# The second quarter of the first tokens: cast during the DMA on GpSimd's queue, or fetched in float32 by SyncE and cast by GpSimd

## The chip, the cores and the metric

The kernel runs on one core of a Trainium2 chip. The metric is the device time of one execution in microseconds; the median of 3 runs of the kernel before is 680.97 us (680.66 to 681.43). A core has a matrix engine (TensorE, PE in the profile; its weight loads are PEld), a vector engine (VectorE, DVE), a scalar engine (ScalarE, ACT), GpSimd (POOL) and SyncE (SP), which only issues DMAs here. All run beside each other, each in its own program order, and wait for each other by semaphores. On chip there are SBUF, 128 partitions of working memory, and PSUM, into which TensorE writes.

## What is computed

A softmax over seven taps for each of eight heads weighs a causal convolution along the sequence; its result goes through a two-layer network with a leaky ReLU.

```python
w = exp(weight - max(weight)); w = w / (sum(w) + 1e-9)          # [8 heads, 7 taps]
x_pad = concat(zeros(B, 6, D), x)                               # x: [8, 4096, 192] float32
out[b, s, h, :] = sum_k w[h, k] * x_pad[b, s + k, h, :]         # a head has 24 of 192 channels
h = out.reshape(32768, 192) @ w_in                              # w_in [192, 2048]
y = maximum(0.01 * h, h) @ w_out                                # w_out [2048, 192], y float32
```

## The kernel before

The tokens are taken in blocks of 512 positions of two batch rows at once (NBLK = 32 blocks). The convolution wants channels on the partitions, so x is brought into a transposed layout, `xt`: 64 channels of one batch row on the lower 64 partitions, the same channels of the other row on the upper 64, for each of three groups of channels (NCH = 3, CH = 64). For each group of tokens there follow the convolution into `yt` (VectorE, L222 and L228; for the first tokens partly TensorE with diagonal matrices, L259), mm1 (`w_in` against `yt`, L507) into PSUM, the leaky ReLU by ScalarE into `g` (L515), and mm2 (`g` with `w_out`; L525 for the first two blocks, L588 after) with its evacuation and output DMA. The program order is written out by hand: mm2 of earlier tokens stands between the mm1 steps of later ones, and VectorE makes the next group's `yt` in the meantime.

The first block's tokens go in halves, so that TensorE can begin early: `groups` has four parts of 256 positions (the parts q = 0 to 3 of the helpers; parts 0 and 1 are block 0), then whole blocks. How a part comes into `xt` differs:

- Part 0: SyncE fetches it in float32 into `x_nat` (L142, two DMAs, one for each `s`, 128 positions). ScalarE and VectorE cast it into `x_half[0]` (`cast_first`, L155), in which the 64 channels of both batch rows lie side by side, and six matmuls against the identity transpose it (L181).
- Parts 1 and 2: two DMAs each on GpSimd's queue, which cast to bfloat16 on the way, into `x_rows[q]` (L145). The two batch rows lie apart there, so `transpose_first` takes 64 columns at a time: twelve transposes (L167). VectorE copies the result from PSUM into `xt` (`evac_first`, L195).
- Part 3: six DMAs on GpSimd's queue (L149), then DMA transposes on SyncE's queue (L199).

Later blocks: six casting DMAs each on GpSimd's queue (L96), then DMA transposes on SyncE's (L114).

GpSimd's program order at the start: the selection matrix; `w_in` rows 0 to 127 of the first half of the columns (L316, `load_w_in(0, 0)`); the identity; `load_w_in(0, 128, near)`; part 1 of x; `load_w_in(0, 128, far)`; the two loads of the second half of `w_in`; part 2 of x; the two halves of `w_out` (L350); the taps for VectorE, `wk` (L445, L446); part 3; block 2. SyncE's: part 0; then, at 18.12 us, the DMA transposes of part 3; then outputs and further transposes.

VectorE's order around the change: evacuation of part 1's transposes (L195), a spreading copy of `w_in` (L326), the first three jobs of part 1's convolution of channel group 1 (L222, L228, which read `wk`), then the spreading of the second half of `w_in` (`spread_down(1)`, L322; `spread_up`, L326), then the further jobs. The spreading copies put rows of `w_in` on the partitions where mm1 wants them. In mm1 of the very first step (`wide`), `transpose_first(1)` stands between the channel groups 1 and 2 (L501, L502): TensorE goes on to group 2 only behind part 1's transposes.

`sync(ins, after, why)` (L78) makes one instruction wait for another.

Of the kernel before, what the change touches and what calls it, by code (L numbers as in the profile page):

```python
# [10 lines left out]
FP32 = mybir.dt.float32  # L11
BF16 = mybir.dt.bfloat16
# [3 lines left out]
def kernel(  # L16
# [8 lines left out]
    nc = tc.nc  # L25

    B, S, D = x.shape
# [8 lines left out]
    CH = 64  # L36
    NCH = D // CH
# [3 lines left out]
    HS = SUB // 2  # L41
    NFC = F // 128
# [3 lines left out]
    RUN = 4  # L46
# [10 lines left out]
    const_pool = ctx.enter_context(tc.tile_pool(name="const", bufs=1))  # L57
    stage_pool = ctx.enter_context(tc.tile_pool(name="stage", bufs=2))
# [17 lines left out]
    x_nat, x_bf, xt = {}, {}, {}  # L76

    def sync(after, first, why):  # L78
        tc.add_manual_dep(
            after.ins, first.ins.name,  # L80
            mybir.DependencyInfo(
                mybir.DependencyClass.Sync, mybir.DependencyReason.DATA
            ),
            reason=why,
        )
# [36 lines left out]
    def new_xt(rp):  # L122
        xt[rp] = xt_pool.tile([128, NCH, HALO + S], BF16, name="xt")
        nc.vector.memset(xt[rp][:, :, 0:HALO], 0.0)
# [3 lines left out]


    x_half = {  # L130
        q: const_pool.tile([128, NCH, HS, 2, CH], BF16, name=f"x_half{q}") for q in (0, 3)
    }
    x_rows = {
        q: const_pool.tile([128, 2, HS, D], BF16, name=f"x_rows{q}") for q in (1, 2)
    }

    def load_first(q):
        rows = x[0:2, q * HT : (q + 1) * HT, :].rearrange("e (s p) d -> p e s d", s=HS)
        if q == 0:
            x_nat[q] = stage_pool.tile([128, 2, HS, D], FP32, name="x_nat")  # L140
            for s in range(HS):
                nc.sync.dma_start(out=x_nat[q][:, :, s], in_=rows[:, :, s])  # L142
        elif q in x_rows:
            for e in range(2):
                nc.gpsimd.dma_start(out=x_rows[q][:, e], in_=rows[:, e])  # L145
        else:
            for c in range(NCH):
                for e in range(2):
                    nc.gpsimd.dma_start(  # L149
                        out=x_half[q][:, c, :, e, :],  # L150
                        in_=rows[:, e, :, c * CH : (c + 1) * CH],
                    )

    def cast_first(q, s, copy, e=slice(0, 2)):
        copy(  # L155
            out=x_half[q][:, :, s, e, :],
            in_=x_nat[q][:, e, s, :].rearrange("p e (c k) -> p c e k", c=NCH),
        )
# [3 lines left out]
    def transpose_first(q, mid=None):  # L162
        if q:
            t = psum_o.tile([128, HS, NCH, 128], BF16, name="ptr", tag="po")
            for s, c in product(range(HS), range(NCH)):
                for e in range(2):
                    nc.tensor.transpose(  # L167
                        out=t[e * CH : (e + 1) * CH, s, c, :],
                        in_=x_rows[q][:, e, s, c * CH : (c + 1) * CH],
                        identity=ident,  # L170
                    )
            ptr[q] = [t[:, s] for s in range(HS)]
            return
        ts = [
            psum_o.tile([128, NCH, 128], FP32, name=f"ptr{s}", tag="po") for s in range(HS)
        ]
        for s, t in enumerate(ts):
            if s and mid is not None:
                mid()
            for c in range(NCH):  # L180
                nc.tensor.matmul(  # L181
                    out=t[:, c, :],
                    lhsT=x_half[q][:, c, s, :, :].rearrange("p e k -> p (e k)"),
                    rhs=ident,
                    start=True,
                    stop=True,
                )
        ptr[q] = ts
# [46 lines left out]
    def y_of(grp, c):  # L235
        blk, t0, T = grp
        if blk not in yt:
            yt[blk] = yt_pool.tile([128, NCH, ST], BF16, name="yt")
        return yt[blk][:, c, t0 : t0 + T]
# [47 lines left out]
    w9 = const_pool.tile([H, K + 1], FP32, name="w9")  # L287
    nc.scalar.dma_start(out=w9[:, 0:K], in_=weight)  # L288
    load_first(0)

    ones = nc.const_aps.tensor(1.0, [128, ST], BF16)
# [7 lines left out]
    for sign, off in ((1, 0), (-1, GRP - 1)):  # L299
        nc.gpsimd.affine_select(  # L300
            out=sel[:, :, 0, :], in_=sel[:, :, 0, :], compare_op=mybir.AluOpType.is_ge,
# [12 lines left out]
    def load_w_in(n, rows, cols=slice(0, WF)):  # L314
        ps, slot = ((0, 128), 0) if rows == 0 else ((0, CH), 2)
        nc.gpsimd.dma_start(  # L316
            out=w_in[n][ps[0] : ps[1], slot, cols],
            in_=moe_w_in[rows : rows + ps[1], n * WF + cols.start : n * WF + cols.stop],
        )
# [17 lines left out]
    ident = const_pool.tile([128, 128], BF16)  # L337
    make_identity(nc, ident)
    load_w_in(0, 128, near)
    load_first(1)  # L340
    load_w_in(0, 128, far)
    for rows in (0, 128):
        load_w_in(1, rows)
    load_first(2)


    w_out = const_pool.tile([128, NFC, D], BF16)
    for h in range(2):
        cs = slice(h * NFC // (2 * RUN), (h + 1) * NFC // (2 * RUN))
        nc.gpsimd.dma_start(  # L350
            out=w_out.rearrange("p (c i) d -> p c i d", i=RUN)[:, cs],
            in_=moe_w_out.rearrange("(c p i) d -> p c i d", p=128, i=RUN)[:, cs],
        )


    wa = psum_h.tile([128, 2, ST], FP32, name="warm", tag="ph")
# [1 line left out]
    def warm(n, cols=HT, to=wa[:, 0]):  # L358
# [10 lines left out]
        out=nmax, in_=w9[:, 0:K], axis=mybir.AxisListType.X,  # L369
# [3 lines left out]
        out=w9[:, 0:K], in_=w9[:, 0:K], func=mybir.ActivationFunctionType.Exp,  # L373
# [18 lines left out]
    def select(out, parts):  # L392
# [9 lines left out]
    select(wps_hm, slice(0, 2))  # L402
    wps_hm = wps_hm[:, :, 0]
    new_xt(0)
    cast_first(0, 0, nc.scalar.copy)
    cast_first(0, 1, nc.scalar.copy, slice(0, 1))
    cast_first(0, 1, nc.vector.tensor_copy, slice(1, 2))
    taps = const_pool.tile([128, NCH, 2, K + 1, 2], BF16, name="taps")
    nc.vector.tensor_copy(
        out=taps, in_=wps_hm[..., None].to_broadcast([128, NCH, 2, K + 1, 2])  # L410
# [5 lines left out]
    def diag_wide(c, p):  # L416
# [8 lines left out]

    warm(1, 192)
    transpose_first(0, lambda: select(wps_l, slice(2, 3)))
    wps_l = wps_l[:, :, 0, 0]
    warm(1, ST, wps[:, 1])
# [9 lines left out]
        out=rsum, in0=wml[:, :, K:], scalar=1e-9, in1=taps[:, :, 0, K:, 0],  # L439
# [14 lines left out]
    def act_scale(out, in_, scale):  # L454
# [11 lines left out]
        out=y_of(groups[0], 0), in0=hi[:, :HT], scalar=rsum[:, 0, :], in1=low,  # L466
# [21 lines left out]
    def mm1(grp, u, M):  # L488
# [11 lines left out]
        for i, c in order:  # L500
            if wide and (i, c) == (0, 2):  # L501
                transpose_first(1)  # L502
            f = nf * u + i
            for e in range(2):
                ps = slice(e * CH, (e + 1) * CH)
                for m in range(0, 128, M):
                    nc.tensor.matmul(  # L507
                        out=ph[m : m + M, e, i * T : (i + 1) * T],
                        lhsT=w_in_of(f, e, c, m, m + M),
                        rhs=y[ps, c, t0 : t0 + T],  # L510
                        start=(c == chunks[0] and not (wide and i)),
                        stop=(c == chunks[-1]),
                        skip_group_check=wide,
                    )
# [155 lines left out]
    for i, grp in enumerate(groups):  # L670
# [11 lines left out]
        for j in range(steps):  # L682
            early = between.get((i, j), (0, 0))
            for u in range(2 * j, 2 * j + 2):
                mm2_slots(i, early[u % 2])
                mm1(grp, u, 128 if i <= NSW else CH)
                if i == 0 and u == 0:
                    evac_first(1, nc.vector.tensor_copy, nc.vector.tensor_copy)
                    spread_up(0, slice(2, 3), far)
                    conv_1 = conv_jobs(groups[1], (1,))  # L690
                    run([conv_1[:3]])
                    spread_down(1)
                    spread_up(1, slice(0, 1), near)
                    spread_up(1, slice(2, 3))
                    run([conv_1[3:5]])
                    spread_up(1, slice(0, 1), far)
                    run([conv_1[5:]])
                    pe_0, evac_0 = pe_conv_jobs(groups[1], 0)
                    pe_2, evac_2 = pe_conv_jobs(groups[1], 2, cross=True)
                if i == 0 and u in CUTS:  # L700
                    cut = slice(*CUTS[u])
                    run(pe_0[cut], pe_2[cut])
                if i == 0 and u == 5:
                    evac_0(nc.vector.tensor_scalar_mul)
                    evac_2(nc.vector.tensor_scalar_mul, nc.vector.tensor_scalar_mul)
                if i == 0 and u == 6:
                    transpose_first(2)
                    evac_first(2, nc.vector.tensor_copy, nc.vector.tensor_copy)
# [59 lines left out]
```

## Time and profile before

| what | us |
|---|---|
| median of 3 runs | 680.97 |
| span of the profiled execution, first to last instruction | 679.2 |
| TensorE busy in it | 674.9 |
| VectorE busy | 481.2 |
| ScalarE busy | 517.6 |
| GpSimd busy | 147.4 |
| first transposes of part 0 (L181) | at 4.01 |
| first mm1 (L507) | at 8.09 |
| transposes of part 1 (L167) | at 8.65 |
| transposes of part 2 (L167) | at 15.98 |
| first mm2 (L525) | at 17.12 |

DMAs of the first stretch, by their issue and their time to landing: x_nat of part 0 at 0.81 and 1.31 us on SyncE's queue, 2.6 us each; part 1 (x_rows) at 3.62 and 4.34, 3.9 and 3.7 us; part 2 at 6.64 and 7.36, 6.6 and 6.5 us; w_out at 8.05 and 8.75, 7.7 and 8.8 us.

In the profile, each line of a timeline gives the start, the time until the last of its instructions ends, the engine, the source line, the operation, what it writes and reads with the shape, and how many instructions it merges; in brackets stands how long the engine was idle before and what ended that. A chain of waits is followed back from the last instruction: at each step to what released it. Of the DMA queues, `software_dynamic` is the one that GpSimd issues to, `hardware_dynamic` SyncE's.

### The profile page before, as it was taken

The page shows a single profiled execution, that of the slowest core. Times are in us where ns is not written, and L with a number is a line of the kernel's source. Part 1 is how long each engine was busy: PE and PEld are TensorE (multiplying, and loading weights), DVE is VectorE, ACT ScalarE, POOL GpSimd, SP SyncE. Part 2 cuts the span into 40 slices and gives each one's busy share as a digit, 9 for nine tenths or more (in the row PEclk, how much of TensorE's full clock was granted, in tenths as well). Part 3 has the DMA queues.
Part 4 walks back from the last instruction along what each step waited for, and adds up shares of the span by engine and source line. Part 5 has one row for each costly group of instructions (what it writes and reads, how often), then busy time and mean ns, then how long its engine had stood idle before and what let it go on. Part 6 is the DMA issues. An engine that isn't in the chain of part 4 may idle for free.

```text
span 679.2 us, 27092 instructions
## 1 busy us (share of the span) xinstructions
PE 674.9 (99%) x12442; PEld 446.3 (66%) x12442; DVE 481.2 (71%) x816; ACT 517.6 (76%) x601; POOL 147.4 (22%) x208
## 2 busy tenths in 40 slices
PE   9999999999999999999999999999999999999998
PEld 6997666666666666666666666666666666666667
DVE  7989477866768766778667687667786676876612
ACT  7899877777787777777777777778777777777781
POOL 8455221122211222211222112222022220000000
PEclk9999999999999999999999999999999999999999
DMA  9999755655737656556556566567365573321123
GB/s 149 99 119 104 52 85 83 84 64 67 96 74 93 76 54 86 84 85 86 66 63 92 80 92 78 56 83 94 73 87 69 60 96 71 72 56 33 34 49 94
DMA packets 213970, 53.27 MB, mean 78 GB/s; under 512 B 209312, under 2 KB 213536, under 8 KB 213856
## 3 DMA queue, kind: packets, MB, share of 16 engines
q0 software_dynamic: 98832, 13.97, 30.3%
q1 hardware_dynamic: 115008, 37.57, 28.0%
q8 instruction: 97, 1.59, 0.9%
q14 instruction: 17, 0.14, 0.1%
q10 hardware_dynamic: 16, 0.00, 0.0%
HBM read 28.31 MB, written 25.17 MB: 79 GB/s over the span
## 4 chain that ended last, share of the span: by engine, by line
PE 98%; DVE 1%; ACT 0%; issue 0%; ACTq 0%
PE ph L507 49%; PE acc L588 44%; PE po L525 5%; PE acc L259 0%; DVE diag L420 0%; PE ptr L167 0%; ACT L366 0%; ACTq L288 0%; DVE w_in L322 0%; DVE yt L465 0%; DVE o_sb L638 0%; DVE x_half L155 0%; ACT w L372 0%; DVE w_in L326 0%; ACT junk L366 0%
## 5 line engine op out<-in xcount | busy, mean ns | idle before, releaser
L515 ACT ACTIVATE g<-ph 128x1024 bf16<-128x1024 f32 x512 | 496.6, 1021 | 139.8 <-PE ph L507 139.6
L228 DVE SCALAR_TENSOR_TENSOR yt<-xt,wk,yt 128x512 bf16<-128x512 bf16 (+1 forms) x582 | 380.1, 715 | 0.2
L507 PE MATMUL ph<-yt,w_in 64*64 64x512 bf16 (+2 forms) x6048 | 377.5, 369 | 0.3 <-DVE yt L465 0.3
L588 PE MATMUL acc<-g,w_out 64*64 64x512 bf16 x5568 | 339.9, 376 | 0.0
L507 PEld LDWEIGHTS <-w_in 64*64 64x64 bf16 (+1 forms) x6048 | 229.7, 131 | 103.4 <-issue 1.1
L588 PEld LDWEIGHTS <-w_out 64*64 64x64 bf16 x5568 | 178.2, 118 | 118.8
L96 POOL DMA_DIRECT2D x_bf<-in_x_dram x180 | 133.9, 774 | 407.6 <-DMA xt<-x_bf 405.6
L610 DVE STREAM_TRANSPOSE o_t<-acc 128x512 f32<-128x512 f32 x87 | 72.9, 875 | 182.2 <-PE acc L588 182.2
L525 PE MATMUL po<-w_out,g 64*128 64x192 bf16 (+1 forms) x640 | 36.8, 243 | 0.0
L525 PEld LDWEIGHTS <-g 64*128 64x128 bf16 (+1 forms) x640 | 32.6, 95 | 3.2 <-issue 0.4
L222 DVE TENSOR_SCALAR yt<-xt,wk 128x512 bf16<-128x512 bf16 (+1 forms) x97 | 28.8, 320 | 2.4 <-DMA xt<-x_bf 2.4
L598 ACT COPY junk<-junk 128x1 f32<-128x1 f32 x58 | 11.1, 191 | 4.1
L638 DVE COPY o_sb<-po 128x192 f32<-128x192 f32 x8 | 2.8, 356 | 6.8 <-PE po L525 3.9
L638 ACT COPY o_sb<-po 128x192 f32<-128x192 f32 x16 | 5.1, 323 | 0.3
L259 PE MATMUL acc<-xt,diag 64*64 64x256 bf16 x126 | 4.7, 272 | 0.1
L149 POOL DMA_DIRECT2D x_half<-in_x_dram x6 | 4.3, 732 | 0.9 <-DMA w_in<-in_moe_w_in_dram 0.9
L259 PEld LDWEIGHTS <-diag 64*64 64x64 bf16 x140 | 3.7, 106 | 1.0 <-issue 0.4
L360 PE MATMUL warm<-const-bfloat16-1.0 128*128 128x512 bf16 (+2 forms) x8 | 3.3, 577 | 0.8 <-PEq L752 0.8
L145 POOL DMA_DIRECT2D x_rows<-in_x_dram x4 | 2.9, 746 | 0.0
L316 POOL DMA_DIRECT2D w_in<-in_moe_w_in_dram x5 | 2.9, 593 | 0.0
L360 PEld LDWEIGHTS <-const-bfloat16-1.0 128*128 128x128 bf16 x10 | 1.2, 128 | 2.2 <-issue 2.2
L326 DVE COPY w_in<-w_in 64x512 bf16<-64x512 bf16 (+1 forms) x7 | 2.3, 337 | 0.2
(52 smaller groups left out, 25.9 us busy)
## 6 DMA issues: line engine op xcount, KB each, us to landing
out_dram<-o_t SPq DMA_DIRECT2D x112, 192.0 KB, 4.7
x_bf<-in_x_dram POOLq DMA_DIRECT2D x180, 64.0 KB, 3.1
out_dram<-o_sb SPq DMA_DIRECT2D x8, 192.0 KB, 2.8
xt<-x_bf SPq DMA_TRANSPOSE x90, 3.2
w_out<-in_moe_w_out_dram POOLq DMA_DIRECT2D x2, 384.0 KB, 8.3
out_dram<-o_t SPq DMA_DIRECT2D x8, 96.0 KB, 2.4
out_dram<-o_sb SPq DMA_DIRECT2D x8, 96.0 KB, 1.7
w_in<-in_moe_w_in_dram POOLq DMA_DIRECT2D x2, 256.0 KB, 5.5
```

What stands on the lines that cost most here:

```text
L96: ins = nc.gpsimd.dma_start(out=t[:, c, :, e, :], in_=src[2 * rp + e, :, :, c * CH : (c + 1) * CH],)
L222: lambda s=src, d=dst, c=c: nc.vector.tensor_scalar_mul(d, s, wk[:, c, 0:1])
L228: lambda s=src, d=dst, c=c, k=k: nc.vector.scalar_tensor_tensor(out=d, in0=s, scalar=wk[:, c, k : k + 1], in1=d, op0=mybir.AluOpType.mult, ...
L259: lambda k=k, p=p, a=a, ps=ps, to=to, acc=accs[e]: nc.tensor.matmul(out=acc[to, :T], lhsT=diag[c][ps, p, k, :], rhs=xt[0][ps, c, a : a + T ...
L360: nc.tensor.matmul(out=to[:, 0:cols], lhsT=ones[:, 0:128], rhs=ones[:, 0:cols], start=True, stop=True,)
L507: nc.tensor.matmul(out=ph[m : m + M, e, i * T : (i + 1) * T], lhsT=w_in_of(f, e, c, m, m + M), rhs=y[ps, c, t0 : t0 + T], start=(c == chun ...
L515: act = nc.scalar.activation(out=g[blk][:, nf * u : nf * (u + 1), :, t0 : t0 + T], in_=ph.rearrange("p e (i t) -> p i e t", i=nf), func=my ...
L525: return nc.tensor.matmul(out=po[m], lhsT=g[b][ps, fc, e, s * 128 : (s + 1) * 128], rhs=w_out[ps, fc, :], start=start, stop=stop,)
L588: ins = nc.tensor.matmul(out=acc2[gi, r][e * CH : (e + 1) * CH, 0:T], lhsT=w_out_of(ps, fc, r), rhs=g[b][ps, fc, e, t0 : t0 + T], start=fi ...
L598: seal = nc.scalar.copy(out=junk, in_=junk)
L610: nc.vector.transpose(out=osb[gi, 0][:, 0 : T // GB, :, r], in_=acc2.pop((gi, r))[:, 0:T].rearrange("p (j k) -> p j k", k=GB),)
L638: ins = copy(out=o_sb[:, n % 2, :], in_=po.pop(n))
```

## The change

Part 1 is fetched like part 0: in float32, by two DMAs on SyncE's queue (one for each batch row, `e`), into a second `x_nat` tile. The first of them waits for ScalarE's first cast of part 0. GpSimd casts it in two instructions (one for each `s`, 128x384, each of which reads what both DMAs bring) into a tile `x_half[1]` with both batch rows side by side, and `transpose_first(1)` takes 128 columns at a time: six transposes. Part 1's two DMAs leave GpSimd's queue, so the loads behind them move up. The two `w_out` loads move behind the two casts in GpSimd's order. Part 2 stays as it was.

```diff
     x_half = {
-        q: ... for q in (0, 3)
+        q: ... for q in (0, 1, 3)
     }
     x_rows = {
-        q: ... for q in (1, 2)
+        q: ... for q in (2,)
     }

-    def load_first(q):
+    def load_first(q, after=None):
...
+        elif q in (1,):
+            x_nat[q] = stage_pool.tile([128, 2, HS, D], FP32, name="x_nat")
+            for e in range(2):
+                ins = nc.sync.dma_start(out=x_nat[q][:, e], in_=rows[:, e])
+                if e == 0:
+                    sync(ins, after, "behind a nearer part")
         elif q in x_rows:
...
     def cast_first(q, s, copy, e=slice(0, 2)):
-        copy(
+        return copy(
             out=x_half[q][:, :, s, e, :],
             in_=x_nat[q][:, e, s, :].rearrange("p e (c k) -> p c e k", c=NCH),
         )
...
             for s, c in product(range(HS), range(NCH)):
+                if q == 1:
+                    nc.tensor.transpose(
+                        out=t[:, s, c, :],
+                        in_=x_half[q][:, c, s].rearrange("p e k -> p (e k)"),
+                        identity=ident,
+                    )
+                    continue
                 for e in range(2):
...
     load_w_in(0, 128, near)
-    load_first(1)
     load_w_in(0, 128, far)
     for rows in (0, 128):
         load_w_in(1, rows)
     load_first(2)
-    w_out = const_pool.tile([128, NFC, D], BF16)
-    for h in range(2):
-        ...
-        nc.gpsimd.dma_start(out=w_out..., in_=moe_w_out...)
...
     new_xt(0)
-    cast_first(0, 0, nc.scalar.copy)
+    after = cast_first(0, 0, nc.scalar.copy)
+    load_first(1, after)
     cast_first(0, 1, nc.scalar.copy, slice(0, 1))
     cast_first(0, 1, nc.vector.tensor_copy, slice(1, 2))
+    for s in range(HS):
+        cast_first(1, s, nc.gpsimd.tensor_copy)
+    w_out = const_pool.tile([128, NFC, D], BF16)
+    for h in range(2):
+        ...
+        nc.gpsimd.dma_start(out=w_out..., in_=moe_w_out...)
     taps = const_pool.tile([128, NCH, 2, K + 1, 2], BF16, name="taps")
```

More of the change, by code (lines that the diff above doesn't have):

```diff
@@ L130 @@
     x_half = {
-        q: const_pool.tile([128, NCH, HS, 2, CH], BF16, name=f"x_half{q}") for q in (0, 3)
+        q: const_pool.tile([128, NCH, HS, 2, CH], BF16, name=f"x_half{q}") for q in (0, 1, 3)
     }
     x_rows = {
-        q: const_pool.tile([128, 2, HS, D], BF16, name=f"x_rows{q}") for q in (1, 2)
+        q: const_pool.tile([128, 2, HS, D], BF16, name=f"x_rows{q}") for q in (2,)
     }
-    def load_first(q):
+    def load_first(q, after=None):
         rows = x[0:2, q * HT : (q + 1) * HT, :].rearrange("e (s p) d -> p e s d", s=HS)
@@ L344 @@
     load_first(2)
-    w_out = const_pool.tile([128, NFC, D], BF16)
-    for h in range(2):
[L349 to L353, printed above, removed]
     wa = psum_h.tile([128, 2, ST], FP32, name="warm", tag="ph")
@@ L404 @@
     new_xt(0)
-    cast_first(0, 0, nc.scalar.copy)
+    after = cast_first(0, 0, nc.scalar.copy)
+    load_first(1, after)
     cast_first(0, 1, nc.scalar.copy, slice(0, 1))
     cast_first(0, 1, nc.vector.tensor_copy, slice(1, 2))
+    for s in range(HS):
+        cast_first(1, s, nc.gpsimd.tensor_copy)
+    w_out = const_pool.tile([128, NFC, D], BF16)
+    for h in range(2):
+        cs = slice(h * NFC // (2 * RUN), (h + 1) * NFC // (2 * RUN))
+        nc.gpsimd.dma_start(
+            out=w_out.rearrange("p (c i) d -> p c i d", i=RUN)[:, cs],
+            in_=moe_w_out.rearrange("(c p i) d -> p c i d", p=128, i=RUN)[:, cs],
+        )
     taps = const_pool.tile([128, NCH, 2, K + 1, 2], BF16, name="taps")
```

## The prediction

> **What bounds the kernel now.** I read the page's busy lines and the shares of the chain that ended last first.
>
> ```profile
> span 679.2 us, 27092 instructions
> PE 674.9 (99%) x12442; PEld 446.3 (66%) x12442; DVE 481.2 (71%) x816; ACT 517.6 (76%) x601; POOL 147.4 (22%) x208
> PE 98%; DVE 1%; ACT 0%; issue 0%; ACTq 0%
> ```
>
> TensorE is the bound: it is idle for 679.2 - 674.9 = 4.3 us in all. What the change touches lies in the first 18 us. From there on TensorE runs in program order nearly without a gap, so a microsecond that it loses there is lost at the end, and little can be won back. So I went on to the same chain in order of time, from 0 to 18 us (start, length, what):
>
> ```profile
> 8.09 0.63 PE ph L507 x8
> 8.72 0.46 PE ptr L167 x12
> 9.18 1.00 PE ph L507 x16
> 10.18 0.78 PE acc L259 x24
> ...
> 13.07 1.68 PE ph L507 x24
> ```
>
> The twelve transposes of the second part (L167) stand in TensorE's stream inside the very first mm1, and everything behind them waits for them. A matmul group of 24 takes 1.31 us later on; the one at 13.07 takes 1.68, so some 0.37 us is waiting, and the waits name DVE w_in L326 for it. Next the timelines of POOL and of DVE:
>
> ```profile
> 3.62 1.44 POOL L145 DMA_DIRECT2D x_rows<-in_x_dram  x2
> 5.03 1.67 POOL L316 DMA_DIRECT2D w_in<-in_moe_w_in_dram  x3
> 6.64 1.48 POOL L145 DMA_DIRECT2D x_rows<-in_x_dram  x2
> 8.05 1.48 POOL L350 DMA_DIRECT2D w_out<-in_moe_w_out_dram  x2
> 9.46 0.32 POOL L445 TENSOR_TENSOR wk<-taps,wml 128x21 f32<-128x21 bf16 x1
> 9.87 0.22 POOL L446 TENSOR_TENSOR wk<-wk,rsum 128x21 f32<-128x21 f32 x1
> ```
>
> ```profile
> 10.26 0.29 DVE L222 TENSOR_SCALAR yt<-xt,wk 128x256 bf16<-128x256 bf16 x1
> 10.59 1.00 DVE L228 SCALAR_TENSOR_TENSOR yt<-xt,wk,yt 128x256 bf16<-128x256 bf16 x2
> 12.21 0.42 DVE L322 COPY w_in<-w_in 64x1024 bf16<-64x1024 bf16 x1 [0.61 <-DMA w_in<-in_moe_w_in_dram]
> 12.64 0.77 DVE L326 COPY w_in<-w_in 64x512 bf16<-64x512 bf16 x2
> ```
>
> POOL never waits here; wk is done at 9.87 + 0.22 = 10.09, and DVE takes it up 0.17 later. Three jobs end at 11.60; then DVE waits 0.61 for w_in and spreads it until 13.41, which is what TensorE waits for.
>
> **The change, part by part.** Four things follow: when the new x_nat lands, when POOL's casts end (call it E), what TensorE waits for, and what DVE waits for.
>
> Removed: two x_rows DMAs on POOL (1.41 us to the next issue), so the three w_in loads and the third part's two loads are issued 1.41 earlier, at 3.62 to 6.71. Twelve transposes in 0.46 us become six of 128 columns; the row of L181 has three such in 4.63 - 4.46 = 0.17, so six take 0.34, a gain of 0.12, where TensorE is what others wait for.
>
> *Landing of x_nat.* Its issue waits for ScalarE's cast of the first part, which starts at 3.44 and takes 0.51, so it starts at 4.00; SP has nothing else to do until 18.12, so nothing queues behind that wait. The first part's x_nat was issued at 0.81, and the windows show the first packets in 1.5 to 2.0, some 1.0 later: the new packets start at 5.0. Landing took 2.6 us for the first part, with the engines free: that would be 4.45 + 2.6 = 7.05. But from 4 to 9 us the DMA engines are full (share 0.96 to 1.35) with POOL's w_in. So what matters is how the two queues share an engine. Three stretches of half a microsecond (packets, MB, share of the engines): x_nat alone (2.5 to 3.0), w_in alone (8.0 to 8.5), and output with x_bf (32.25 to 32.75; two lines):
>
> ```profile
> q1 hardware_dynamic: 252, 0.18, 108.7%
> ...
> q0 software_dynamic: 44, 0.09, 117.0%
> ...
> q1 hardware_dynamic: 109, 0.08, 66.8%
> q0 software_dynamic: 123, 0.02, 47.8%
> ```
>
> Together, the queues move almost as many packets each (109 and 123), although one's are 768 B and the other's 128 B; the packets' start times in the trace repeat every 58 ns on both. So the share is one packet for one packet. That is bad for x_nat: half a microsecond is 8 us of 16 engines, so its 768 B packet takes 8/238 = 0.034 us of one (14 of the 252 are small), the w_in packet of 2,048 B 8/44 = 0.182. It has 512 packets, 32 on each of 16 engines. In POOL's new order there stand against it, per engine: 4 + 4 packets of 1,024 B (half of 0.182 each: 0.73 us), 8 and 4 of 2,048 B (2.18 us), then the third part's packets of 384 B (the second part's move at 201 in 6.25 to 6.75: 0.040 each). Twenty x packets pass with those twenty, the last twelve with twelve small ones (0.48). Sum 0.73 + 2.18 + 0.48 + 32 x 0.034 = 4.5 us: last packet at 9.5, landing 0.3 later, 9.8. Bounds: 7.05 (no contention) and 10.5 (another 0.7, as the engines' dip to a share of 0.50 at 10.0 to 10.5 would cost). I take 9.8, since the two-queue row is the nearest.
>
> The Trainium skill ("DMA: Bandwidth & Descriptors", section "Queues, rings and completion order") has an engine drain a packet of some 9 to 17 descriptors before it switches. By that rule x_nat would need two turns with one turn of POOL's between them, 5.0 + 0.54 + 2.2 + 0.54 + 0.3 = 8.6, and the sum below would end near 682.1; equal counts alone would fit that too, the 58 ns do not.
>
> *The casts.* Both read both halves, so they start at landing. No row shows POOL copying float32. Nearest: its affine selects, 128x192 in 0.36 and 128x128 in 0.29, 1.1 ns a column: 384 columns give 0.58. Bounds: 0.35 (DVE's cast of half as many columns) and 1.15 (twice the 0.58, for twice the bytes). E = 9.8 + 2 x 0.58 = 10.95 (8.3 with the early landing; 7.75 and 12.8 at the ends).
>
> *TensorE.* Its last three transposes start 0.05 after E and end at 11.17; before, mm1 went on at 9.11. So it stands for some 2.06.
>
> *POOL and DVE behind the casts.* Queued behind the waiting cast on POOL are w_out (1.41 to the next, 0.63 from 9.46 to the end of wk): wk is done at E + 2.04 = 13.0 in place of 10.09. DVE's first job follows at E + 2.2, its three jobs take 1.34, so spreading starts at E + 3.55 = 14.5 in place of 12.21: 2.3 late. w_in is then long there (its packets are through at about 8.2), so the 0.61 wait goes, and wk is late in its place. TensorE reaches that mm1 about 2 us late and waits for the rest. The two delays lie beside each other; the larger counts: E - 8.66 = **+2.3 us**.
>
> *Covers.* w_out is issued 2.9 later. Its landing took 7.7 and 8.8, behind the queue; with the same times it lands at 18.65 and 20.5, while mm2 wants it at 17.12 + 2.3 = 19.4 and, for the second half, 19.09 + 2.3 = 21.4. That holds, by 0.8; without the cover each microsecond costs one. The fourth part's loads come 2.9 later, but their transposes end at 23.3 and DVE wants them at 25.65 + 2.3. Later loads of x hang on SP's and TensorE's own progress.
>
> Sum: 679.2 + 2.3 = 681.5 span. The median 680.97 is 1.8 above the profiled span; with the same 1.8, 683.3.
>
> **The rivals.** (1) *The transfer is not held up*: SP's queue gets its packets through as for the first part. Place: the landing before L167. E is 8.3, TensorE's transposes are hardly delayed, wk comes at 10.35, DVE's 0.61 wait is used up, and E - 8.66 = -0.3: 680.7, no change. It decides when the landing is before 7.5; up to 8.8 the loss stays within 0.2%. For it: 2.6 us in the only row of this very load. Against it: that row had the engines to itself. (2) *POOL's casts are long*: 1.15 each in place of 0.58 adds 1.1: 684.5. For it: float32 input was not seen on POOL; against it: ScalarE does the same cast in 0.51. (3) *Less w_in waiting wins*: with an early landing, TensorE's 0.37 at 13.07, the 0.12 of the transposes and a few waits of 0.2 go. That is under 1 us, 680.0; a gain of more than 0.2% (1.4 us) finds no wait in the chain that could pay for it.
>
> **How the numbers follow.** 0.2% is about what a measurement of this kernel can tell from no change. Forecast (landing 8.8 to 10.5): 0.60, 683.3. Rival 1 with the middle landings, and rival 3 as far as it stays within 0.2%: 0.27. Rival 2: 0.09. Something that wins over 0.2%: 0.04. Slower 0.60 + 0.09 = 0.69, same 0.27, faster 0.04. The forecast's own range is 682.3 to 684.0; the whole one goes from rival 1 to rival 2: 680.7 to 684.5.
>
> **What would show it.** In the profile after: landing of x_nat 5 us or more after its issue (rival 1: under 3); POOL waiting for DMA x_nat until about 9.8; two POOL casts of some 0.58; PEld or PE waiting for POOL x_half at the transposes for about 2 us; six transposes in 0.34; DVE L222 waiting for POOL wk, and no wait of L322 for w_in. A landing before 8 would make the prediction wrong, and so would a TensorE that reaches the transposes later for another reason, such as w_in delayed by x_nat.

## The result and the profile after

The changed kernel takes 687.60 us (median of 4 runs, 687.28 to 687.89) against 681.11 for the kernel before in the same series: 6.5 us more, a ratio of 1.0097 with a 95% interval of 1.0083 to 1.0110. The forecast was 683.3, its range ended at 684.5. The sign was right, the size was not. The profiled execution has a span of 686.2 us, 7.0 more than that of before.

The page's first lines, and its row of granted clock (40 slices of 17 us; an 8 is under full speed):

```profile
span 686.2 us, 27083 instructions
PE 677.1 (99%) x12436; PEld 450.1 (66%) x12436; DVE 480.4 (70%) x816; ACT 517.7 (75%) x601; POOL 147.2 (21%) x208
PEclk8999999999999999999999999999999999999999
```

TensorE is idle for 9.1 us in place of 4.3, and busy 2.2 us longer although it has six instructions fewer. The chain that ended last, in order of time:

```profile
4.38 8.22 DMA x_nat<-in_x_dram
...
12.74 0.51 POOL x_half L161
13.25 0.05 issue
13.30 0.95 PE ptr L173 x6
14.25 1.82 PE ph L520 x16
16.08 1.43 PE acc L272 x20
```

Where TensorE's own work stood from 8 us on, there is now a DMA: the second x_nat transfer lands 8.2 us after its issue, at 12.6. GpSimd casts, and only then do the transposes start, at 13.30 in place of 8.65. And what follows is slow: 16 matmuls of mm1 take 1.82 us, where they took 1.00 before. GpSimd's timeline and then VectorE's, behind the casts:

```profile
12.74 0.95 POOL L161 CAST x_half<-x_nat 128x384 bf16<-128x384 f32 x2 [6.08 <-DMA x_nat<-in_x_dram]
13.64 1.41 POOL L417 DMA_DIRECT2D w_out<-in_moe_w_out_dram  x2
15.05 0.26 POOL L458 TENSOR_TENSOR wk<-taps,wml 128x21 f32<-128x21 bf16 x1
```

```profile
15.65 0.29 DVE L235 TENSOR_SCALAR yt<-xt,wk 128x256 bf16<-128x256 bf16 x1 [0.42 <-POOL wk L459]
15.97 1.00 DVE L241 SCALAR_TENSOR_TENSOR yt<-xt,wk,yt 128x256 bf16<-128x256 bf16 x2
17.00 0.42 DVE L335 COPY w_in<-w_in 64x1024 bf16<-64x1024 bf16 x1
```

The brackets tell the story of the queue: GpSimd waited 6.08 us for x_nat, VectorE then 0.42 for wk, and its old wait for w_in is gone. The last view is of four stretches of 3.41 us (TensorE's busy time, weight loads, VectorE, ScalarE, GpSimd, then granted clock, DMA share, GB/s), cut where the trace has the clock change:

```profile
4.51:7.92 3.41, 3.19 (x94) 2.77 (x93) 3.30 (x13) 2.01 (x6) 2.15 (x4) 1.00 0.85 138
7.92:11.33 3.41, 0.72 (x8) 0.26 (x7) 0.94 (x3) 1.41 (x3) 0.00 (x0) 1.00 1.09 201
11.33:14.75 3.41, 1.45 (x12) 0.92 (x14) 0.46 (x2) 0.00 (x0) 2.00 (x4) 0.50 0.24 31
14.75:18.16 3.41, 3.41 (x46) 2.06 (x42) 2.85 (x8) 2.05 (x2) 3.33 (x7) 0.50 0.97 152
```

While TensorE stood, its clock was cut to half, and it worked at half speed until 18.16. So there are two things to explain: a landing at 12.6 in place of 9.8, and a clock that the forecast did not reckon with.

### The profile page after: what moved, and what is told of

Same layout as the page of the kernel before. It is cut to its first block, busy times and chain, and to the rows that moved or that the text cites. A ratio compares the mean times of both kernels' runs of the same rounds, so it can differ in the third digit from the quotient of the medians.

```text
span 686.2 us, 27083 instructions
## 1 busy us (share of the span) xinstructions
PE 677.1 (99%) x12436; PEld 450.1 (66%) x12436; DVE 480.4 (70%) x816; ACT 517.7 (75%) x601; POOL 147.2 (21%) x208
## 4 chain that ended last, share of the span: by engine, by line
PE 98%; DMA 2%; ACT 0%; POOL 0%; DVE 0%; issue 0%; SPq 0%; POOLq 0%
PE ph L520 49%; PE acc L601 44%; PE po L538 5%; DMA x_nat<-in_x_dram 2%; PE acc L272 0%; PE ptr L173 0%; ACT x_half L161 0%; POOL x_half L161 0%; PE ptr L180 0%; DVE o_sb L651 0%; SPq L146 0%; POOLq L161 0%
## 5 line engine op out<-in xcount | busy, mean ns | idle before, releaser
L601 PEld LDWEIGHTS <-w_out 64*64 64x64 bf16 x5568 | 180.9, 119 | 116.5
```

The lines of the kernel that those rows point to most:

```text
L601: ins = nc.tensor.matmul(out=acc2[gi, r][e * CH : (e + 1) * CH, 0:T], lhsT=w_out_of(ps, fc, r), rhs=g[b][ps, fc, e, t0 : t0 + T], start=fi ...
```

## The experiments

Theory Q at the start: x_nat takes turns, packet for packet, with GpSimd's queue. It became theory T: x_nat lands when GpSimd's queue is through, and each load in that queue adds its own engine time. Theory K: the half clock adds about 2 us to what the late casts cost. The rivals are named in the quoted expectations. Times are medians; "before" is the kernel before in the same series. In the table, landing and E, the end of the casts, are those of the one profiled execution. As in the prediction, the second part is q = 1 and the third q = 2.

| kernel | landing | E | time | before |
|---|---|---|---|---|
| changed kernel | 12.6 | 13.7 | 687.60 | 681.11 |
| the same, a second series | 11.6 | 12.7 | 687.69 | 681.15 |
| no wait for ScalarE's cast | 8.2 | 9.4 | 681.76 | 681.17 |
| zero matmuls in the gap | 12.1 | 13.2 | 685.89 | 681.17 |
| the same, second series | 12.3 | 13.4 | 685.70 | 681.15 |
| far, second w_in half, third part held | 8.1 | 9.2 | 685.47 | 681.17 |
| all four loads held | 7.7 | 8.8 | 686.02 (one run) | 681.15 |
| second half of w_in held | 9.8 | 10.9 | 684.86 | 681.03 |
| third part held | 11.3 | 12.4 | 687.12 | 681.03 |
| packets of twice the size | 12.1 | 13.2 | 686.58 | 681.17 |
| fetch on GpSimd's queue | 8.4 | 9.5 | 681.54 | 681.03 |
| the same, one cast on ScalarE | 8.3 | 9.1 | 681.46 | 680.86 |
| before, with an idle fetch | (9.9) | - | 682.89 | 681.03 |

### Holding GpSimd's loads back

In the changed kernel, loads on GpSimd's queue are moved behind the two casts, so that x_nat does not meet them.

```diff
     load_w_in(0, 128, near)
-    load_w_in(0, 128, far)
-    for rows in (0, 128):
-        load_w_in(1, rows)
-    load_first(2)
...
     for s in range(HS):
         cast_first(1, s, nc.gpsimd.tensor_copy)
+    load_w_in(0, 128, far)
+    for rows in (0, 128):
+        load_w_in(1, rows)
+    load_first(2)
```

> The changed kernel with GpSimd's far half of w_in rows 128 to 191, the second half of w_in and the third part's loads moved behind the two casts, so that x_nat meets only the end of the first w_in loads. Theory Q: landing at about 7.1, 2.7 us after its issue, casts done at 8.2, the transposes not held up; the held loads and wk come 3 us late instead, so 683 to 684.5 us. Rival P (a fetch on SyncE's queue at this place is slow by itself, whatever GpSimd's queue holds): landing at 11 or later, 689 or more.

The chain's line for the second x_nat transfer (start, length):

```profile
4.41 3.66 DMA x_nat<-in_x_dram
```

It lands at 8.07, 4.5 us earlier than in the changed kernel. So a fetch at this place is not slow by itself: rival P falls. It is not 7.1 either: a full microsecond is left. The held loads cost elsewhere as expected, and more: TensorE waits 2.27 us for the spreading of the late w_in, and there, in the profiled execution, the clock falls again.

Two kernels hold one kind of load each: the second half of w_in alone (put straight behind the casts), or the third part alone (behind wk).

> The changed kernel with the two loads of the second half of w_in (192 packets of 2,048 B, 2.2 us of each engine) moved behind the casts; the far load and the third part's loads stay in front. Theory T and Rival W: landing at about 9 to 10, casts done by 10 to 11; the late w_in then arrives at about 15 to 16, so 684 to 687 us. Rival I: landing at 11.5 or later.

> The changed kernel with the third part's two loads moved behind wk, so that GpSimd writes no descriptors from 5.2 to 6.7 and 64 small packets of an engine fewer stand in its queue; the w_in loads stay. Theory T (every packet of GpSimd's queue costs x_nat its own time on the slowest engine, 1.3 us of them here): landing at about 11 to 11.6 in place of 12.6, 686 to 687 us. Rival I (x_nat is held up by GpSimd's work on descriptors more than by the packets): landing at 10 or earlier, 683 to 685. Rival W (only w_in's large packets count): landing unchanged.

The chain of the one without the second half of w_in:

```profile
4.19 5.65 DMA x_nat<-in_x_dram
```

Without w_in's second half the landing is at 9.84, 1.8 to 2.8 earlier than in the two series of the changed kernel (11.6 and 12.6). Without the third part it is at 11.34, 0.3 to 1.3 earlier: that fits the 32 x 0.040 us of an engine that its packets take, but alone it does not exclude rival W, by which only w_in's large packets count. Against rival W stands the kernel without w_in's second half: it lands 1.77 later than the one of the first experiment (8.07), with the far load (0.36) and the third part (1.28) added in front. Rival I falls: it wanted 10 or earlier without the third part and 11.5 or later without w_in's second half, so GpSimd's work on descriptors (the orders that it writes for the DMA engines) between 5.2 and 6.7 is not what mainly holds x_nat up. The last kernel of this kind holds the near load as well:

> The changed kernel with the near load of w_in held behind the casts as well, so that x_nat meets the end of the first w_in load alone. Theory T: another 0.4 us earlier than with the near load, landing at 7.6; and if every packet in the other queue costs its own time, nothing else is left in it. Rival S (SyncE's queue starts late by itself here): landing stays at 8.0 to 8.1. The time is no help here: the near load lands at 12 or later and mm1 starts 4 us late.

```profile
4.41 3.28 DMA x_nat<-in_x_dram
```

It lands at 7.69, 0.38 before the one with the near load, whose packets take 0.36. Now the sum can be made. With the engine times of the prediction's rows (near 0.36, far 0.36, second half of w_in 2.18, third part 1.28) on top of 7.69: with near 8.05 (measured 8.07), with near, far and third part 9.69 (9.84), with near, far and w_in 10.59 (11.34), with all 11.87 (11.6 and 12.6 in two series). For these kernels the rule holds to 0.8 us; it is a fit, with its base taken from one of them, and it fails for a fetch below.

### The size of the packets

The second part's positions are laid out so that each packet of x_nat is 1,536 B (this permutes the second part's positions in the result).

```diff
+            rows = x[0:2, q * HT : (q + 1) * HT, :].rearrange("e (p s) d -> p e s d", s=HS)
             x_nat[q] = stage_pool.tile([128, 2, HS, D], FP32, name="x_nat")
```

> The changed kernel with two neighbouring positions on one partition in the second part, so that each packet of x_nat is 1,536 B in place of 768: the same bytes in half as many packets (the second part's positions come out permuted, so its results are not the reference's). Theory Q with one-for-one turns: 16 packets of an engine pass with 16 of GpSimd's in place of 32, landing at 9.5 to 11 in place of 12.6, 683.5 to 685.5 us. Rival B (the queues share by bytes or by time): landing stays at 12 to 13, 687 to 688.

The landing stays at 12.1, inside what the unchanged kernel shows: half the turns were not half the wait. The time, 686.58, lies between the two forecasts. From 8 to 9 us the two queues move almost one for one:

```profile
q0 software_dynamic: 58, 0.10, 54.0%
q1 hardware_dynamic: 52, 0.07, 28.7%
```

But that is no rule. In the changed kernel SyncE's and GpSimd's queue move 104 and 56 packets from 6 to 7 us, 117 and 64 from 8 to 9, 118 and 128 from 9 to 10, 70 and 246 from 10 to 11. And x_nat's first packet moves at 6.0, where the prediction has 5.0. The changed kernel from 5 to 6 us:

```profile
q0 software_dynamic: 123, 0.12, 87.7%
q1 hardware_dynamic: 1, 0.00, 0.3%
```

With all four loads held it is 26 and 192 in that microsecond, and x_nat begins at 5.1. So theory Q's equal share holds for some microseconds and not for the transfer. A mean engine also seems the wrong one to count. Each of the two x_nat transfers has 16 packets of 4 B, which I read as one at the end of each engine's share; the later 16 of the 32 lie between 9.5 and 12.3 in the changed kernel, and between 6.9 and 7.7 in the kernel of the first experiment. By this reading the landing is the slowest engine's. What makes some engines slow, no run here tells; it stays open. A second queue is not needed for it: in the kernel before, a w_in load of 256 KB landed 6.6 us after its issue while SyncE's queue moved nothing, and its own packets take 8 x 0.182 = 1.5 us of an engine.

### A fetch that nobody waits for

The kernel before, with the change's fetch added behind ScalarE's cast, into a tile that nothing reads.

```diff
+    after = cast_first(0, 0, nc.scalar.copy)
+    rows = x[0:2, HT : 2 * HT, :].rearrange("e (s p) d -> p e s d", s=HS)
+    idle = stage_pool.tile([128, 2, HS, D], FP32, name="x_nat")
+    for e in range(2):
+        ins = nc.sync.dma_start(out=idle[:, e], in_=rows[:, e])
+        if e == 0:
+            sync(ins, after, "behind a nearer part")
```

> The kernel before with an additional fetch, the change's two float32 DMAs on SyncE's queue behind ScalarE's first cast, into a tile that nothing reads; so 3.1 MB of reads become 3.5 in the first 18 us, and nothing waits for it. Theory T, seen from the other side: the fetch lands at 11 to 13 here too, and GpSimd's loads give back as much: the second part's x_rows land at 9 to 10 in place of 8.0, the transposes come 0.5 to 1.5 us late, 681.7 to 682.7 us. Rival (SyncE's packets take the back seat and cost the other queue nothing): x_rows at 8.0, time as before, 681.2.

From 7.5 to 8.5 us, the second part's 384 B packets on one queue and the idle fetch's 768 B on the other:

```profile
q0 software_dynamic: 181, 0.07, 63.0%
q1 hardware_dynamic: 162, 0.12, 49.1%
```

Almost one for one again, in this microsecond. But alone, the prediction's rows give 402 and 476 of these in a microsecond: 181/402 + 162/476 = 0.79. Together the queues moved a fifth less than these rates let expect. The chain shows who paid:

```profile
4.33 6.03 DMA x_rows<-in_x_dram
10.36 0.04 issue
10.40 0.52 PE ptr L167 x11
```

x_rows lands at 10.36 in place of 8.04, the transposes are done 1.7 us late, and the kernel takes 1.9 us more (ratio 1.0032, 1.0022 to 1.0042). The fetch itself landed at 9.9, earlier than expected; the queue it disturbed lost more than I had thought. Theory T's sum fails here: 7.69 + 0.36 + 1.28 + 0.36 + 2.18 + 1.28 = 13.15, 3.3 more than measured. A fetch on the second queue at this place is a loss even when nothing needs it. Whether the same additional bytes on GpSimd's queue would cost as much was not tried.

### The same fetch at other places

Without the wait, SyncE issues the fetch right behind the first part's, at 1.8 and 2.3 us.

```diff
     load_first(0)
+    load_first(1)
...
-    load_first(1, after)
```

> The changed kernel with the wait taken away: SyncE issues the second part's two fetches right behind the first part's, at 1.8 and 2.3 us. Theory Q (x_nat is late because its packets take turns, one for one, with the w_in packets of GpSimd's queue, and the slowest of the 16 engines sets the landing): they stand behind the first part's packets until 3.5 and then meet w_in all the same; landing at 9 to 11 us, casts done at 10 to 12, 682.5 to 684.5 us, clock not dropped or hardly. Rival W (the wait for ScalarE's cast is what makes it late): landing by 6 to 7, the transposes not held up, 680.7 us.

It lands at 8.2: earlier than theory Q expected, later than rival W wanted (6 to 7). The time, 681.76, lies between the two as well. Its price is VectorE's line:

```profile
7.93 0.29 DVE L340 COPY w_in<-w_in 64x512 bf16<-64x512 bf16 x1 [1.37 <-DMA w_in<-in_moe_w_in_dram]
```

The first w_in load lands 6.05 us after its issue in place of 4.5, and the first mm1 starts at 9.09 in place of 8.09. Of that, 0.6 us is left at the end (ratio 1.0010, 1.0001 to 1.0020). The bytes are the same; what is needed next is late either way.

On GpSimd's own queue, at the place where the part's loads stood before (`load_first` issues from GpSimd, still in float32):

```diff
     load_w_in(0, 128, near)
+    load_first(1)
...
-    load_first(1, after)
```

> The changed kernel with x_nat fetched in float32 by GpSimd's own queue, at the place where the part's loads stood before; GpSimd's casts, the six wide transposes and the order casts, w_out, wk stay. If SyncE's queue is the whole cause: landing at 7.5 to 8, as the part had before, casts done at 9.0, the transposes at most 0.3 us late, wk at 11.0, so +0.4 us: 681.5. If the casts, the wide transposes or the place of w_out cost by themselves: 683 or more.

```profile
4.35 4.02 DMA x_nat<-in_x_dram
...
9.57 0.34 PE ptr L171 x3
```

It lands at 8.37, the casts end at 9.51, and the kernel takes 681.54: ratio 1.0005, 0.9996 to 1.0013, no difference that can be told. The float32 fetch, GpSimd's casts, the wide transposes and w_out's new place together cost 0.5 us by the medians, and no more than 0.9 by the interval. The other 6 us come with the fetch's place: on SyncE's queue, and issued beside the w_in loads that on GpSimd's own queue stand behind it. Which of the two counts for how much is not separated: a fetch on GpSimd's queue behind those loads was not tried, and the one that SyncE issues ahead of them cost 0.6. Last, the same with one cast on ScalarE (ahead of its copies that spread the first half of w_in) and w_out behind wk:

```diff
-    for s in range(HS):
-        cast_first(1, s, nc.gpsimd.tensor_copy)
+    cast_first(1, 0, nc.gpsimd.tensor_copy)
...
+    cast_first(1, 1, nc.scalar.copy)
```

> The kernel with the float32 fetch on GpSimd's queue, its second cast given to ScalarE (ahead of ScalarE's spreading copy) and w_out moved behind wk, so that wk waits for one cast alone. By the sum of the prediction with the casts done at 9.0 to 9.3 in place of 9.5 and wk at 9.7: TensorE goes on at 9.4 to 9.5 (0.3 late, taken back at the mm1 that waits for w_in), w_out lands 0.2 to 1 us before mm2 wants it; 681.0 to 681.4, no difference to before that can be measured. If the half microsecond of the kernel it is built on came from w_out's place and not from the casts: unchanged at 681.5; if w_out is now too late: 682 or more.

681.46 against 680.86 (ratio 1.0009, 1.0000 to 1.0018). TensorE went on at 9.52 as expected, 0.34 late, but only 0.14 of that was taken back: the mm1 that waited for w_in took 1.54 in place of 1.68. No kernel here beats the one before.

### The clock

Into the gap of the changed kernel go 20 matmuls with zero weights, added onto mm1's running sums.

```diff
             if wide and (i, c) == (0, 2):
+                for _ in range(20):
+                    nc.tensor.matmul(
+                        out=ph[:, 0, :], lhsT=zero, rhs=ones[:, 0:ST],
+                        start=False, stop=False, skip_group_check=True,
+                    )
                 transpose_first(1)
```

> The changed kernel with 20 matmuls of 512 columns with zero weights, added onto mm1's sums ahead of the second part's transposes: they change no value and keep TensorE busy for some 4.3 us of the 4.6 that it stands. Theory K (the clock that fell to half from 11.3 to 18.2 us costs what the late casts alone don't explain): granted clock 1.00 throughout, transposes still wait until about 13.3, time 686.1 us by the waits alone (casts done at 13.7, 5.0 us late). Rival (the half clock is hidden behind VectorE and GpSimd, which are late anyway): 687.4 to 687.7.

The time was 685.89, but x_nat had also landed 0.5 us earlier. So it went with the changed kernel into one more series:

> The kernel of the 20 zero matmuls once more, against the changed kernel of the same series. Theory K: clock 1.00, landing as there; 1.2 to 2.0 us faster than the changed kernel, with the rest of the loss (4.5 to 5 us) left. If the first comparison owed its 1.7 us to an earlier landing alone, the difference goes to 0.5 or less.

> The changed kernel once more, beside its own variant with the filling matmuls. Theory T (x_nat lands when the whole of GpSimd's queue is through): landing at 12 to 13, granted clock at half for some 3.4 to 6.8 us, 687 to 688 us.

685.70 (685.64 to 685.94) against 687.69 (687.18 to 687.97): 2.0 us faster, although x_nat landed 0.7 later than in the profiled execution beside it. The stretch from 11 to 12 us, with TensorE busy throughout and the clock at 1.00:

```profile
11.00:12.00 1.00, 1.00 (x7) 0.46 (x5) 0.00 (x0) 0.00 (x0) 0.00 (x0) 1.00 0.62 76
```

The prediction's sum, E - 8.66, separates the two parts. With the filling matmuls the spans of two profiled executions are 4.6 and 4.8 over before's 679.2, and E - 8.66 gives 4.5 and 4.7: 0.1 is left. For the changed kernel, 7.0 and 6.3 against 5.0 and 4.1: 2.0 and 2.2 us are left, and they are the clock's. The chains agree without that sum. In the filled kernel (the one with the 20 matmuls) mm1's 16 matmuls behind the transposes are

```profile
13.71 0.99 PE ph L527 x16
```

in place of 1.82; the next two groups take 0.78 and 1.44 in place of 1.43 and 1.75. That is 1.8 us, and the transposes are shorter too (0.34 in place of 0.95). Theory K holds.

## Why the prediction was wrong

- **Which wait ends last**: right for the casts. TensorE waits for GpSimd's casts, they for x_nat; and on VectorE wk takes the place of the wait for w_in. But behind the casts the chain runs through TensorE alone, at half clock: it reaches the mm1 that needs the spread w_in 6.9 us late (19.93 for 13.07), when the spreading is only 4.8 late (17.00 for 12.21), and that mm1 takes 1.56 in place of 1.68. So the late wk cost nothing there.
- **The sum behind the casts**, E - 8.66: right on VectorE within 0.24 us. With E = 13.69 it has wk done at 15.73 (measured 15.61), VectorE's first job at 15.89 (15.65), the spreading at 17.24 (17.00). On TensorE it was short: mm1 was to go on at E + 0.22 and goes on at E + 0.56, with all six transposes behind the first cast and at half clock (E + 0.40 at full clock, with the fetch on GpSimd's queue). The two profiled executions of the filled kernel agree with E - 8.66 within 0.1 us; in the first, TensorE goes on 4.53 late (13.71 for 9.18) and the spreading is 4.3 late, so the two delays do lie beside each other. A slip in the prediction's sums: the early landing gives E = 7.05 + 2 x 0.58 = 8.2, not 8.3; nothing turns on it.
- **The casts**: 0.58 each, measured 0.50. Six wide transposes at full clock: 0.34, measured 0.36.
- **The cover of w_out**: it held. The two halves landed 4.5 and 6.1 us after issue, long before mm2.
- **The landing of x_nat**: the step that failed. "Sum 0.73 + 2.18 + 0.48 + 32 x 0.034 = 4.5 us: last packet at 9.5, landing 0.3 later, 9.8", and it was 12.6. Two of its terms can be read in the trace. The start: x_nat's first packet moved at 6.0 and not at 5.0, behind a microsecond in which GpSimd's queue moved 123 packets and SyncE's 1. The passing: the last packet moved at 12.2, 6.2 us after the first in place of 4.5. The turns that it stood on are one for one in some microseconds (181 and 162) and not in others (104 and 56, 70 and 246), and only 12 of the third part's 32 packets on an engine were counted (0.48). The fit over the held kernels divides the same 2.8 us in another way. The base is 5.0 + 1.08 + 0.3 = 6.4 by the prediction's terms without any other load, and the kernel with all four held shows 7.69, 1.3 more (the first w_in load still moves there, and the sum left it out). The third part counted whole (1.28) is 0.8 more. The last 0.7 no term gives; the changed kernel's own series differ by 1.0. Why the passing takes that long stays open; that the slowest engine sets it is a reading of the trace and not shown by a run. The upper bound of 10.5 was a guess at one dip, although the trace of before had the w_in load that landed 6.6 us after its issue.
- **The clock**: not in the sum nor among the rivals. A stall of 2.06 us was forecast, and its price taken as its length.
- Put together: 7.0 us of span against 2.3 forecast, of which 2.7 come from the landing (E 13.69 in place of 10.95) and 2.0 from the clock.
- **The rivals**: the first (no hold-up) was contradicted by the fetch beside a full queue; long casts by 0.50 us; and nothing was won, since what early w_in could have given (0.37 us) lay behind the same wait. The rule of the Trainium skill that the prediction weighed ("DMA: Bandwidth & Descriptors", section "Queues, rings and completion order"), whole packets of 9 to 17 descriptors before a switch, would have had x_nat land at 8.6, where the runs with full queues have 11.6 to 12.6. Equal counts, where they are seen (between 384 and 768 B, and between 2,048 and 1,536 B), would fit it as well as single turns, so the counts do not decide between the two; the landing follows from neither.

## What to carry to other kernels

A transfer moved to a second queue does not leave the first queue's way: here it waited for most of the loads in flight beside it, and held them up in turn. So add up the engine time of both queues, and leave room for slow engines; even so the sum was off by up to 0.8 us in one family of kernels and by 3.3 us in another. Before an edit, ask what else is in flight at its issue, and move it alone first (here the same fetch on the old queue cost nothing that can be measured). And price a stall of TensorE of a microsecond or two with the clock that it may lose, not by its length alone.

## What the runs showed of the hardware

- Two queues at once can move fewer packets than either alone would let expect: 0.45 + 0.34 of their rates in the microsecond shown. In the changed kernel the engines were busy for only 63% from 6 to 7 us (56 packets of GpSimd's queue, 104 of SyncE's), though both queues had more to move.
- GpSimd casts 128x384 from float32 to bfloat16 in 0.50 us, as fast as ScalarE (0.51), with VectorE idle.
- The clock is decided in stretches of 3.41 us (it stayed at half for 3.41 or 6.83 us in every profiled execution in which it fell in the first 20 us), and they need not be idle. In the kernel with the idle fetch, TensorE stood for 0.39 us, and then for 0.73 and 0.72 on both sides of one transpose. Its stretches (TensorE busy, clock, DMA share, GB/s):

```profile
7.70:11.11 3.41, 1.58 (x26) 1.00 1.18 196
11.11:14.53 3.42, 3.42 (x46) 0.50 1.28 199
```

The clock fell after stretches with 0.55 to 1.58 us of TensorE's work, and stayed after one with 2.29 (the kernel without the second half of w_in). It came back after a stretch that was busy throughout, and not after one with 2.90 us of work (the kernel without the third part, from 11.53 to 14.94). That fits a stall which costs a clock or not by where it falls among the stretches, though only one run of that kernel, with a fall, was profiled: of the 11 runs with the idle fetch, 8 had a granted clock of 1.000 and took 682.1 to 683.2 us, 3 had 0.995 to 0.997 and took 684.1 to 686.1. The Trainium skill ("TensorE: Matmul & The Clock Gate", section "Part 1: The HAM clock gate (the "warmup" mystery)") gives the same 3.4 us, free-running, but has the clock go back after an idle stretch; here one that was busy for 46% was enough, and the measurement decides.
